# Weights' conversion from float64: a parametric Relu on ScalarE and one VectorE operation less

## The chip, the cores and the metric

One core of a Trainium2 chip runs the whole program. It has a TensorE (PE in the rows; PEld is its weight load), a VectorE (DVE), a ScalarE (ACT), a GpSimd (POOL) and a SyncE (SP) that issues the transfers. The metric is the device time of one execution in microseconds (us), and lower is better.

## The reference, cut to what matters

```python
kv  = einsum('bhsd,bhse->bhde', k, v)          # linear attention, 8 x 8 heads, 576 rows, 64 columns
out = einsum('bhsd,bhde->bhse', q, kv)
x   = out / sqrt(mean(out*out) + 1e-6) * g_norm    # -> 4608 tokens x 512

h = x @ w_in                                    # 512 x 2048
g = (a0 + a1*h + a2*h^2 + a3*h^3) / (1 + |b0||h| + |b1|h^2 + 1e-6)
x = g @ w_out                                   # 2048 x 512

return (((x @ w1) * (x @ w2)) @ w3) @ w_out2    # 512 x 1024 twice, 1024 x 1024, 1024 x 512
```

The activations q, k, v are float32. The six weight matrices are float64, since their float32 draw is scaled by a float64 factor. [...]

## The kernel before, in words

**Conversion.** `raw_load` brings a weight block of 128 x 512 float64 (512 KB) into a tile of pairs of words: `hw` is the high word (sign, 11 exponent bits, 20 mantissa bits) and `lw` the low word. `to_f32` makes a float32 tile `ct` of it in four operations. ScalarE reads `hw` as if it were a float32 and scales it by 2^-112, which corrects the exponent's offset and writes `ct` (line 149). VectorE cuts three bits out of the low word (line 151), shifts `ct` left by three and puts these bits in (line 155, into `lw`), and then puts the sign, which the shift has pushed out, back from the unshifted `ct` (line 159, into `ct`). Two more operations follow for the weights of the first two layers: ScalarE rounds `ct` to the high part (line 84) and VectorE subtracts for the low part (line 85). `conv` puts this pair into a list, `pend`, and `conv_on` runs it two conversions later, at the end of another block's `to_f32`.

**Where conversions stand.** There are 88. (1) 32 blocks of `w_in` (wa0 to wa15) and `w_out` (wb0 to wb15): 11 in an opening that is written out as a string of letters, one by one among the first attention tiles, and 21 in the first steps of the main loop (CONV gives how many in each step). (2) 32 half blocks of 128 x 256 of `w1` and `w2` (`bg_conv`) in the steps 64 and later. (3) 24 blocks of `w3` and `w_out2` (`cv_conv`, tile wb12) in the stage after the main loop.

**The main loop** has 192 steps g. Step g does on TensorE the 12 matmuls of layer one for one block of 128 hidden units and 384 tokens (`l1`, lines 88 to 90, into one of two PSUM tiles `h`), then the 12 of layer two of step g-3 (`l2`, lines 500 to 503), and between them matmuls of the attention of later tokens (lines 286, 347, 360, 403). The rational function is spread over ScalarE (lines 546 to 548, 562, 563, 536), GpSimd (line 550) and VectorE (lines 553, 555, 569, 571, 573, 538). Line 562 of a step waits for GpSimd's product of the same step, and `l1` of step g+2 waits for line 555 of step g, the last reader of that `h`.

**What sets the order.** Every engine works in program order. In a step, `mix` draws from generators in the order of a string; each letter runs one of them to its next `yield`, and what is left over runs at the end:

```python
MIX = "nntltsuysltsttunuuu", "snsnalttaltyasnt", "ntsnnltlsyttst"
```

The first string is for the steps with conversions of (1): n is lines 546 to 555, t, u and v are conversions, l the split of lines 536 and 538, y lines 562 and 563, s lines 569 to 573. The second is for those of (2). The opening runs each conversion as a whole.

Of the kernel before, what the change touches and what calls it, by code (L numbers as in the profile page):

```python
# [12 lines left out]
AF = mybir.ActivationFunctionType  # L13
ALU = mybir.AluOpType
# [4 lines left out]
def linear_attention_two_moe_kernel(  # L19
# [24 lines left out]
    nc = tc.nc  # L44
# [35 lines left out]
    def f32(ap):  # L80
        return ap.bitcast(F32)
# [62 lines left out]
    def to_f32(raw, t, n=W):  # L144


        hw, lw = raw[:, :, 1], raw[:, :, 0]
        ti = t.bitcast(I32)
        nc.scalar.activation(out=t, in_=f32(hw), func=AF.Copy, scale=2.0**-112)
        yield  # L150
        nc.vector.tensor_scalar(
            out=lw, in0=lw.bitcast(U32), scalar1=2.0**-29, scalar2=7.0, op0=ALU.mult, op1=ALU.min
        )
        yield
        nc.vector.scalar_tensor_tensor(
            out=lw, in0=ti, scalar=3, in1=lw, op0=ALU.logical_shift_left, op1=ALU.bitwise_or
        )
        yield
        nc.vector.scalar_tensor_tensor(
            out=ti, in0=ti, scalar=-0x80000000, in1=lw, op0=ALU.bitwise_and, op1=ALU.bitwise_or  # L160
        )

    def f32_tile(n=W):
# [16 lines left out]
    def conv(raw, *stages):  # L180

        t = f32_tile(W)
        yield from to_f32(raw, t)
        pend.append((t, list(stages)))
        conv_on()
# [231 lines left out]
    with tc.manual_schedule():  # L417
# [183 lines left out]
        for i in range(T0, NTILE):  # L601
            j, t = divmod(i, TPB)
# [30 lines left out]
        def bg_conv(n):  # L633
            w = f32_tile(HW)
            yield from to_f32(bg_raw.pop(n), w, HW)
            nc.sync.dma_start(out=bg[n][2], in_=w)
# [223 lines left out]
        def cv_conv(n):  # L860
            w = f32_tile()
            run(to_f32(cv_raw.pop(n), w))
            nc.sync.dma_start(out=cv[n][1], in_=w)
# [525 lines left out]
```

## Time and profile before

| | before |
|---|---|
| time, median of 3 runs (lowest, highest) | 1559.38 us (1557.82, 1559.94) |
| the profiled execution: time, span | 1558.43 us, 1556.7 us |
| TensorE busy, share of the span | 1515.8 us, 97% |
| VectorE | 1243.2 us, 80% |
| ScalarE | 1056.5 us, 68% |
| GpSimd | 225.0 us, 14% |

The span runs from the first instruction to the last. A busy TensorE is not a TensorE at its full rate, since a matmul's end in the trace is modelled, and the shares are means over stages with different limits. So what a VectorE operation is worth has to be read from the stage in which it stands.

### The profile page before, as it was taken

The numbers are of one execution on the slowest core, as the hardware profiler recorded it, in microseconds if no ns is written. First come the engines' busy times: TensorE is split into PE (matmuls) and PEld (weight loads), VectorE is DVE, ScalarE is ACT, GpSimd is POOL, SyncE is SP. The second block draws the span as 40 slices with busy tenths as digits, with TensorE's granted clock in tenths as the row PEclk, the third lists the DMA queues.
The fourth block names the chain that finished last, engine by engine and source line by source line (L and its number), as shares of the span: only waits on it lengthen the run. The fifth ranks groups of instructions, "written<-read, shape, count | busy, mean of one in ns | idle before, by whom it ended". The sixth has DMA issues, their size and how long they took to land.

```text
span 1556.7 us, 26099 instructions
## 1 busy us (share of the span) xinstructions
PE 1515.8 (97%) x9640; PEld 1477.4 (95%) x9640; DVE 1243.2 (80%) x2374; ACT 1056.5 (68%) x2109; POOL 225.0 (14%) x201
## 2 busy tenths in 40 slices
PE   4899999999999999999999999999999999999999
PEld 3788999999999999999999999999999999899999
DVE  5899968777889888988888889877677675688875
ACT  4688877787888888888888888544344343555554
POOL 0122221222222222222222221000000000000000
PEclk9799999999999999999999999999999999999999
DMA  9644243231112111110101021443543534434452
GB/s 281 194 141 140 72 112 99 82 96 45 48 38 69 42 45 42 45 55 28 58 28 56 6 69 37 146 146 112 190 141 117 190 119 164 140 110 154 155 160 89
DMA packets 153456, 157.95 MB, mean 101 GB/s; under 512 B 57328, under 2 KB 131312, under 8 KB 153328
## 3 DMA queue, kind: packets, MB, share of 16 engines
q1 hardware_dynamic: 153328, 156.28, 32.0%
q8 instruction: 76, 1.25, 0.3%
q14 instruction: 52, 0.43, 0.1%
HBM read 106.43 MB, written 49.81 MB: 100 GB/s over the span
## 4 chain that ended last, share of the span: by engine, by line
PE 85%; DVE 9%; ACT 3%; DMA 1%; issue 1%; POOL 1%; SPq 0%; DVEq 0%; POOLq 0%
PE acc L787 11%; PE h L88 8%; PE h L90 8%; PE h L89 8%; PE acc L500 7%; PE acc L501 7%; PE acc L503 7%; PE acc L1045 5%; PE h L787 5%; PE at L787 3%; PE kv L787 3%; PE h L1045 2%; PE kv L1045 2%; PE at L1045 2%; PE at L360 1%
## 5 line engine op out<-in xcount | busy, mean ns | idle before, releaser
L550 POOL TENSOR_TENSOR s<-z,a 128x384 f32<-128x384 f32 x192 | 223.3, 1163 | 732.6 <-ACT z L547 663.4
L553 DVE TENSOR_TENSOR n<-n,h 128x384 f32<-128x384 f32 x192 | 105.5, 550 | 91.9 <-ACT n L548 89.9
L546 ACT ACTIVATE a<-h 128x384 f32<-128x384 f32 x192 | 94.2, 491 | 98.3 <-PE h L90 97.6
L571 DVE SCALAR_TENSOR_TENSOR n<-n,na,y 128x384 f32<-128x384 f32 x192 | 155.4, 809 | 0.0
L562 ACT ACTIVATE y<-s,epsq 128x384 f32<-128x384 f32 x192 | 118.2, 616 | 44.7 <-POOL s L550 43.6
L547 ACT ACTIVATE z<-a,ab 128x384 f32<-128x384 f32 x192 | 136.2, 709 | 6.4
L548 ACT ACTIVATE n<-h,na 128x384 f32<-128x384 f32 x192 | 125.8, 655 | 0.0
L555 DVE SCALAR_TENSOR_TENSOR n<-n,na,h 128x384 f32<-128x384 f32 x192 | 116.4, 606 | 0.5
L569 DVE SCALAR_TENSOR_TENSOR s<-s,y 128x384 f32<-128x384 f32 x192 | 109.3, 569 | 0.0
L538 DVE TENSOR_TENSOR lo<-n,hi 128x384 fp32r<-128x384 f32 x192 | 106.9, 557 | 0.0
L573 DVE SCALAR_TENSOR_TENSOR n<-s,n 128x384 f32<-128x384 f32 x192 | 105.5, 550 | 0.2
L563 ACT ACTIVATE y<-y 128x384 f32<-128x384 f32 x192 | 101.0, 526 | 6.1
L536 ACT CAST hi<-n 128x384 fp32r<-128x384 f32 x192 | 96.1, 500 | 1.1 <-DVE n L573 1.1
L286 PEld LDWEIGHTS kv<-vt,kt 128*64 128x64 f32 (+1 forms) x640 | 24.7, 151 | 25.7 <-DMA kt<-in_k_dram 17.0
L286 PE MATMUL kv<-vt,kt 128*64 128x64 f32 (+1 forms) x640 | 30.4, 243 | 16.2 <-DMA vt<-in_v_dram 16.2
L829 ACT COPY p<-kv 128x384 f32<-128x384 f32 x24 | 11.5, 480 | 38.5 <-PE kv L787 26.9
L829 ACT COPY p<-acc 128x384 f32<-128x384 f32 x24 | 11.5, 480 | 38.5 <-PE acc L787 30.9
L844 ACT COPY u<-acc 128x384 f32<-128x384 f32 x24 | 11.5, 480 | 31.6 <-PE acc L787 31.6
L360 PE MATMUL at<-kvbd,qT 128*128 128x128 f32 (+1 forms) x216 | 29.2, 285 | 3.1 <-DVE kvbd L303 2.7
L360 PEld LDWEIGHTS at<-kvbd,qT 128*128 128x128 f32 (+1 forms) x216 | 26.6, 184 | 5.2 <-POOL s L550 3.0
L844 ACT COPY u<-h 128x384 f32<-128x384 f32 x24 | 11.5, 480 | 28.1 <-PE h L787 26.9
L379 DVE TENSOR_REDUCE ms<-sq 128x8 f32<-128x512 f32 x36 | 24.4, 683 | 5.9 <-ACT sq L373 5.9
(1440 smaller groups left out, 4923.0 us busy)
## 6 DMA issues: line engine op xcount, KB each, us to landing
ed<-eo SPq DMA_DIRECT2D x48, 384.0 KB, 2.6
er<-ed SPq DMA_DIRECT2D x35, 512.0 KB, 3.8
x2d<-xev SPq DMA_DIRECT2D x48, 192.0 KB, 2.0
xr<-x2d SPq DMA_DIRECT2D x48, 192.0 KB, 3.9
out_dram<-o SPq DMA_DIRECT2D x36, 256.0 KB, 2.0
kt<-in_k_dram SPq DMA_DIRECT2D x32, 256.0 KB, 2.8
vt<-in_v_dram SPq DMA_DIRECT2D x32, 256.0 KB, 3.2
qt<-in_q_dram SPq DMA_DIRECT2D x32, 256.0 KB, 3.1
```

The lines of the kernel that those rows point to most:

```text
L88: nc.tensor.matmul(outp, lhsT=lh, rhs=rh, start=first, stop=False)
L89: nc.tensor.matmul(outp, lhsT=lh, rhs=rl, start=False, stop=False)
L90: nc.tensor.matmul(outp, lhsT=ll, rhs=rh, start=False, stop=last)
L547: nc.scalar.activation(out=z, in_=a, func=AF.Identity, scale=ab[:, 1:2], bias=ab[:, 0:1])
L548: nc.scalar.activation(out=n, in_=h, func=AF.Identity, scale=na[:, 3:4], bias=na[:, 2:3])
L550: nc.gpsimd.tensor_tensor(out=s, in0=z, in1=a, op=ALU.mult)
L555: nc.vector.scalar_tensor_tensor(out=n, in0=n, scalar=na[:, 1:2], in1=h, op0=ALU.add, op1=ALU.mult)
L562: nc.scalar.activation(out=y, in_=e["s"], func=AF.Abs_reciprocal_sqrt, bias=epsq[:, 0:1])
L569: nc.vector.scalar_tensor_tensor(out=s, in0=s, scalar=EPS_Q, in1=y, op0=ALU.add, op1=ALU.mult)
L571: nc.vector.scalar_tensor_tensor(out=n, in0=n, scalar=na[:, 0:1], in1=y, op0=ALU.add, op1=ALU.mult)
L787: nc.tensor.matmul(bank, lhsT=lh[:, sl], rhs=x, start=first and kk == 0 and n == 0, stop=kk == 1 and n == 2, skip_group_check=True,)
L1045: nc.tensor.matmul(bank, lhsT=l[:, c, :], rhs=r, start=first and c == 0 and x == 0, stop=c == KH - 1 and x == 2, skip_group_check=True,)
```

## The change

ScalarE's scaling becomes a parametric Relu: inputs above zero are scaled by 2^-112 as before, and inputs below zero by 2^-112 times 2^32. The extra 2^32 adds 32 to a negative number's exponent field, which is bit 28 of the word, and the shift by three moves that bit to the sign's place, bit 31. So one VectorE operation both shifts and joins the low word's bits, and it writes `ct` directly; the second one goes, and with it one `yield`.

```diff
-        nc.scalar.activation(out=t, in_=f32(hw), func=AF.Copy, scale=2.0**-112)
+        nc.scalar.activation(out=t, in_=f32(hw), func=AF.Prelu, scale=2.0**-112, alpha=2.0**32)
         yield
         nc.vector.tensor_scalar(
             out=lw, in0=lw.bitcast(U32), scalar1=2.0**-29, scalar2=7.0, op0=ALU.mult, op1=ALU.min
         )
         yield
         nc.vector.scalar_tensor_tensor(
-            out=lw, in0=ti, scalar=3, in1=lw, op0=ALU.logical_shift_left, op1=ALU.bitwise_or
-        )
-        yield
-        nc.vector.scalar_tensor_tensor(
-            out=ti, in0=ti, scalar=-0x80000000, in1=lw, op0=ALU.bitwise_and, op1=ALU.bitwise_or
+            out=ti, in0=ti, scalar=3, in1=lw, op0=ALU.logical_shift_left, op1=ALU.bitwise_or
         )
```

The instruction lists of TensorE, ScalarE, GpSimd and SyncE are the same in both kernels, row for row (ScalarE's has one table load, at its head, in both). VectorE's has 88 rows less, 2310 against 2222, and in the steps with conversions some rows stand in another order. Lines behind the edit have numbers that are four lower in the changed kernel.

In the opening, this is VectorE's list before from the conversion of block wb1 to the first row sums of the attention tiles (line 379; wa4, wa5, wb0, wb1, wb2 are weight blocks, `r` marks the raw words, `hl` the two parts):

```order
L151 TENSOR_SCALAR wb1r<-wb1r 128x512
L155 SCALAR_TENSOR_TENSOR wb1r<-ct,wb1r 128x512
L159 SCALAR_TENSOR_TENSOR ct<-ct,wb1r 128x512
L85 TENSOR_TENSOR wb0hl<-ct,wb0hl 128x512
L151 TENSOR_SCALAR wa5r<-wa5r 128x512
L155 SCALAR_TENSOR_TENSOR wa5r<-ct,wa5r 128x512
L159 SCALAR_TENSOR_TENSOR ct<-ct,wa5r 128x512
L85 TENSOR_TENSOR wa4hl<-ct,wa4hl 128x512
L151 TENSOR_SCALAR wb2r<-wb2r 128x512
L155 SCALAR_TENSOR_TENSOR wb2r<-ct,wb2r 128x512
L159 SCALAR_TENSOR_TENSOR ct<-ct,wb2r 128x512
L85 TENSOR_TENSOR wb1hl<-ct,wb1hl 128x512
```

In the changed kernel the three rows of line 159 are gone here, and nothing else moves; the row sums of line 379 come next in both.

In the main loop, this is VectorE's list of one step with one conversion, before (step 20; s, n, lo, h are tiles of the rational function, wb14 and wb12 weight blocks):

```order
L151 TENSOR_SCALAR wb14r<-wb14r 128x512
L569 SCALAR_TENSOR_TENSOR s<-s,y 128x384
L571 SCALAR_TENSOR_TENSOR n<-n,na,y 128x384
L538 TENSOR_TENSOR lo<-n,hi 128x384
L155 SCALAR_TENSOR_TENSOR wb14r<-ct,wb14r 128x512
L573 SCALAR_TENSOR_TENSOR n<-s,n 128x384
L159 SCALAR_TENSOR_TENSOR ct<-ct,wb14r 128x512
L85 TENSOR_TENSOR wb12hl<-ct,wb12hl 128x512
L555 SCALAR_TENSOR_TENSOR n<-n,na,h 128x384
```

And the same step in the changed kernel:

```order
L151 TENSOR_SCALAR wb14r<-wb14r 128x512
L565 SCALAR_TENSOR_TENSOR s<-s,y 128x384
L567 SCALAR_TENSOR_TENSOR n<-n,na,y 128x384
L534 TENSOR_TENSOR lo<-n,hi 128x384
L155 SCALAR_TENSOR_TENSOR ct<-ct,wb14r 128x512
L85 TENSOR_TENSOR wb12hl<-ct,wb12hl 128x512
L569 SCALAR_TENSOR_TENSOR n<-s,n 128x384
L551 SCALAR_TENSOR_TENSOR n<-n,na,h 128x384
```

One row is gone, and the subtraction of line 85 now stands ahead of the last operation of the previous step's function (line 573 before, 569 after) instead of behind it.

## Rows read from the trace of the kernel before

**Rows 1.** Busy time by stage: start:end, length, then engines, clock, DMA share, GB/s.

```profile
core 0: us, PE busy (x) PEld busy (x) DVE busy (x) ACT busy (x) POOL busy (x), PEclk, DMA share, GB/s
16.00:48.00 32.00, 17.27 (x127) 14.71 (x128) 29.20 (x56) 19.59 (x39) 0.00 (x0) 0.87 0.89 270
...
87.40:169.30 81.90, 77.03 (x519) 71.03 (x517) 81.05 (x160) 72.65 (x137) 24.20 (x16) 1.00 0.44 135
...
250.00:820.00 570.00, 570.00 (x3530) 560.81 (x3529) 483.97 (x947) 468.07 (x914) 136.85 (x123) 1.00 0.18 53
...
980.00:1290.00 310.00, 310.00 (x1770) 309.88 (x1769) 219.04 (x417) 132.67 (x280) 0.00 (x0) 1.00 0.43 145
```

**Rows 2.** The chain that ended last, 103 to 170 us: shares by line.

```profile
by line: DMA wb14r<-in_moe_w_out_dram 6.5%; DVE n L571 6.3%; DVE n L555 6.3%; DVE ct L159 6.3%; DVE n L573 5.6%; DVE s L569 5.6%; issue 5.1%; POOL s L550 5.0%; DVE lo L538 3.8%; ACT z L547 3.2%; PE h L88 2.9%; ACT y L562 2.6%; ACT y L563 2.
```

**Rows 3.** TensorE's waits up to 160 us: us in total, times, longest.

```profile
PE h L88 <- DVE n L555: 5.8, 7, 2.1
PE acc L403 <- DVE xt L396: 5.3, 2, 3.7
```

**Rows 4.** Lines 149 and 159: nanoseconds least/median/most, first and last start.

```profile
L149 ACT ACTIVATE ct<-wb12r x25: 657/674/695, 150.4 to 1289.0; 128x512 f32<-128x512 f32 x25
...
L159 DVE SCALAR_TENSOR_TENSOR ct<-ct,str x32: 406/418/423, 256.0 to 818.4; 128x256 int32<-128x256 int32 x32
L159 DVE SCALAR_TENSOR_TENSOR ct<-ct,wb12r x25: 684/693/695, 154.6 to 1290.4; 128x512 int32<-128x512 int32 x25
```

**Rows 5.** ScalarE's first and second operation on `h`, groups of the page.

```profile
L546 ACT ACTIVATE a<-h 128x384 f32<-128x384 f32 x192 | 94.2, 491 | 98.3 <-PE h L90 97.6
...
L547 ACT ACTIVATE z<-a,ab 128x384 f32<-128x384 f32 x192 | 136.2, 709 | 6.4
```

**Rows 6.** The opening in order of time: start, duration, [idle before, what ended it].

```profile
29.10 1.12 PE L347 MATMUL acc<-ident,qt 128*128 128x128 f32 x4 [1.64 <-DMA qt<-in_q_dram]
...
30.48 0.68 ACT L149 ACTIVATE ct<-wb2r 128x512 f32<-128x512 f32 x1
...
32.15 0.60 ACT L373 ACTIVATE sq<-h 128x512 f32<-128x512 f32 x1
...
35.29 0.69 DVE L159 SCALAR_TENSOR_TENSOR ct<-ct,wb2r 128x512 int32<-128x512 int32 x1
35.90 0.68 DVE L85 TENSOR_TENSOR wb1hl<-ct,wb1hl 128x512 fp32r<-128x512 f32 x1
36.50 1.27 DVE L379 TENSOR_REDUCE ms<-sq 128x8 f32<-128x512 f32 x2
```

**Rows 7.** Step 1 in order of time: the long line 159 and TensorE's wait.

```profile
57.52 1.38 DVE L159 SCALAR_TENSOR_TENSOR ct<-ct,wb4r 128x512 int32<-128x512 int32 x1
...
64.70 1.94 PE L360 MATMUL at<-kvbd,qT 128*64 128x128 f32 x8 [2.75 <-DVE kvbd L303]
```

**Rows 8.** VectorE, line 555 of two successive steps; nine operations stand between.

```profile
155.80 0.61 DVE L555 SCALAR_TENSOR_TENSOR n<-n,na,h 128x384 f32<-128x384 f32 x1
...
160.86 0.61 DVE L555 SCALAR_TENSOR_TENSOR n<-n,na,h 128x384 f32<-128x384 f32 x1
```

**Rows 9.** Line 546, once a step, from step 6 to step 22.

```profile
L546 ACT ACTIVATE a<-h x17: 474/492/528, 87.4 to 169.3; 128x384 f32<-128x384 f32 x17
```

**Rows 10.** ScalarE in step 19 and the first operation of step 20.

```profile
153.81 0.49 ACT L546 ACTIVATE a<-h 128x384 f32<-128x384 f32 x1 [0.41 <-PE h L90]
...
156.79 0.62 ACT L562 ACTIVATE y<-s,epsq 128x384 f32<-128x384 f32 x1 [0.21 <-POOL s L550]
...
157.87 0.60 ACT L84 CAST wa15hl<-ct 128x512 fp32r<-128x512 f32 x1
158.88 0.50 ACT L546 ACTIVATE a<-h 128x384 f32<-128x384 f32 x1 [0.41 <-PE h L90]
```

**Rows 11.** TensorE's matmuls of line 286, and line 546 of two later steps.

```profile
155.79 0.69 PE L286 MATMUL kv<-vt,kt 128*64 128x64 f32 x16
...
416.90 0.49 ACT L546 ACTIVATE a<-h 128x384 f32<-128x384 f32 x1 [0.23 <-PE h L90]
...
421.10 0.49 ACT L546 ACTIVATE a<-h 128x384 f32<-128x384 f32 x1 [0.61 <-PE h L90]
```

**Rows 12.** Busy time and clock in two short stretches (columns as rows 1).

```profile
39.70:43.10 3.40, 1.83 (x8) 1.43 (x8) 2.97 (x8) 2.16 (x6) 0.00 (x0) 0.50 0.59 196
...
63.60:67.00 3.40, 2.29 (x9) 1.99 (x10) 3.34 (x8) 1.46 (x3) 0.83 (x1) 0.50 0.34 102
```

**Rows 13.** ScalarE's only table load.

```profile
L464 ACT ACT_TABLE_LOAD x1 | 1.3, 1283 | 0.7 <-PEq L1373 0.7
```

## Prediction

> **What bounds the kernel now.** I read the busy time by stage first, since VectorE's 80% is a mean. From 250 to 820 us TensorE is busy without a gap, and so it is from 980 to 1290 [rows 1]. All 32 half-block conversions lie in the first of these, from 256.0 to 818.4, and of the 25 with the tile wb12 one is a block of the second layer, at 154.6, and the 24 others belong to the stage behind the loop, up to 1290.4 [rows 4]. So their second VectorE operation runs beside a TensorE that waits for nothing. In the two earlier stretches it is the other way round: VectorE is busy 29.2 of 32 us from 16 to 48, while TensorE is busy 17.3, and 81.05 of 81.9 us from 87.4 to 169.3 [rows 1]. The reader is to see there an engine without a hole. The chain of work that ended last says the same of 103 to 170 us: line 159, which the change removes, lies on it with 6.3%, among five other VectorE lines [rows 2]. And TensorE's own waits up to 160 us name VectorE: 5.8 us for line 555, which releases an `h`, and 5.3 us for the normalized tile that is transposed first [rows 3]. So 32 of the 88 removed operations stand where VectorE sets the pace.
>
> **The change part by part.**
>
> *What is removed.* One operation of 128x512 costs 0.69 us by its own duration and one of 128x256 0.42 us [rows 4]. 24 of the first kind and all 32 of the second, 24 x 0.69 + 32 x 0.42 = 30 us, stand in the two stretches where TensorE has no gap: worth nothing. Were that cover gone, a step of the background conversions could win 0.42 us at most. The other 32 are counted by place.
>
> *Opening (11 conversions).* Eight of them, wa1 to wa3, wb0, wa4, wb1, wa5 and wb2, are done before the first row sums, which start at 36.50 [rows 6]. Eight times 0.69 would be 5.5 us, but not all can be had. The second row sum needs the square that ScalarE starts at 32.15; that square stands behind the attention matmuls of tile 1, and these behind a transposition that waited until 29.10 for q from DRAM [rows 6]. VectorE's work does not move that. ScalarE's scaling of wb2 starts at 30.48 and takes 0.68, so it ends at 31.16; one shift-and-join (0.69) and one subtraction of line 85 (0.60 from start to start, 35.90 to 36.50) follow, and the pair of row sums can start at 32.5 at the earliest, 4.0 us before now [rows 6]. I take 3.8, because ScalarE has a copy of a tile to do (as long as the square, 0.6) before it can use the first sum. The bounds are 3.0 (a quarter lost to transfers that are as late as now) and 4.0. The other three conversions of the opening end in VectorE's wait for the first step and count nothing; without that wait they would be worth 3 x 0.69.
>
> *Step 0 and 1.* Here the operation of line 159 took 1.38 us, twice its normal time [rows 7]. TensorE then waits 2.75 us for the copy of line 303, which stands behind this operation and the next block's [rows 7]. In the changed list both are gone: 1.38 + 0.69 = 2.1 us less as durations. One of the two lies next to an operation that could be stretched in its place, as line 159 was, so I take 1.6, bounds 0.6 and 2.1; the wait of 2.75 us holds it.
>
> *Steps 6 to 21 (16 steps, 16 conversions).* Line 546 runs once a step; 17 of them lie from 87.4 to 169.3, so a step takes 81.9 / 16 = 5.12 us [rows 9]. VectorE needs 160.86 - 155.80 = 5.06 us for its ten operations [rows 8], so nearly every step is VectorE's. With nine, the removed one counted from start to start as line 85 is (0.60), it needs 4.46. What is next? TensorE: a later step with 24 matmuls and nothing else takes 421.10 - 416.90 = 4.20, and every second step has line 286's matmuls besides, 0.69, so 4.20 + 0.35 = 4.55 [rows 11]. ScalarE: from its first operation at 153.81 to the end of line 84 at 157.87 + 0.60 is 4.66, with a wait of 0.21 for GpSimd inside; the 0.41 idle behind it is a wait for TensorE [rows 10]. So ScalarE's own 4.66 is the new floor of such a step, just above the other two, and the gain is 16 x (5.12 - 4.66) = 7.4 us. The bounds: 9.1 if only TensorE's 4.55 holds (16 x 0.57 = 9.1), and 4.2 with ScalarE at 4.86 (next paragraph). The moved subtraction (line 85 ahead of line 573) delays line 573 by one operation of 0.60 and saves one of 0.60 ahead of it: nothing. Its input, line 84, ends 4.66 us behind the step's start and VectorE gets to it some five us behind it (line 555 of step 19 starts at 160.86, 7.05 behind, three rows later in the new list), so no wait is added. Should ScalarE be late there, lines 573 and 555 queue behind it, and TensorE's `l1` two steps on behind line 555.
>
> *The scaling's new function.* No row has a parametric Relu. The scaling takes 0.674 us [rows 4]. On this engine two operations of one size differ most where one has per-row operands, 491 against 709 ns [rows 5]; the new one has constants alone, so I take 0, with bounds 0 and +0.2 us a conversion. At +0.2 a step of ScalarE takes 4.86. A gain has no ground: the old form is the simplest that there is.
>
> *The clock.* In 39.7 to 43.1 and in 63.6 to 67.0 the granted clock was 0.50, the lower level of 1.2 GHz; TensorE had been idle for 3.7 us before the first [rows 3] and 2.75 us before the second [rows 7, 12]. Both waits are among those that get shorter: the first by most of its length, the second to below 1 us. Twelve matmuls cost 2.1 us at the full clock (half of 4.20) and as much again at half [rows 11]. If both low stretches went, step 0's twelve would give 2.1 and step 3's twelve with the attention matmuls before them (1.94 at half [rows 7]) 2.1 + 1.0 = 3.1, so 5.2 in all; 0 if the clock falls as before. I take 1.5, half of the second.
>
> *Sum.* 3.8 + 1.6 + 7.4 + 1.5 = 14.3 us. Against the profiled execution, 1558.43, that is 1544.1; the median of the runs is 0.95 higher, so 1545.1.
>
> **The rivals.**
>
> *ScalarE and GpSimd hold the steps.* If the new function costs 0.2 more, the steps give 16 x (5.12 - 4.86) = 4.2, and with the opening at 3.8, step 1 at 0.6 and no clock, the gain is 8.6: 1550.8. For it: ScalarE is busy 72.65 of 81.9 us there [rows 1]. Against it: nothing but the function's table changes.
>
> *The clock stays up.* 3.8 + 2.1 + 7.4 + 5.2 = 18.5: 1540.9. For it: shorter waits. Against it: TensorE still waits in both places.
>
> *No change.* If the opening were paced by the transfers (DMA share 0.89 [rows 1]) and the steps by ScalarE at 5.0 or more, less than 3 us would be left: 1557 to 1559. Against it: VectorE has no idle time in the steps, and ScalarE waits in each [rows 10].
>
> *Table loads, slower.* If the parametric Relu is not in the table set in which the reciprocal square root is, each conversion needs a load before and one after it, at 1.28 us each [rows 13]. ScalarE's step would be 4.66 + 2.57 = 7.23 and the 16 steps 2.1 us longer each, 34 us; in a step of the background conversions ScalarE's 4.20 - 0.61 idle = 3.59 [rows 11] becomes 6.16, 32 x 1.96 = 63 us; so 1559.4 + 97 = 1656, and more with the opening. It decides from about seven such steps on (14.3 / 2.1). Against it: the changed ScalarE list has one load, at its head, as before. The Trainium skill (ScalarE activation tables: per-element evaluation and per-set limits, What a function is on this engine) has it that two functions of different sets are one load of 1283 ns apart, that those of one set need no switch, and that the same operands cost the same whichever table is read. The first figure is that of this trace's one load [rows 13]; by the last the +0.2 above would be nothing, and the sum would stay; no row here shows a parametric Relu.
>
> **How the numbers follow.** The forecast, gain 10 to 17, has 0.64; ScalarE's rival 0.14; the clock's 0.14; no change 0.05; table loads 0.03. The range takes in the first three: low, 1559.4 - 20.4 (4.0 + 2.1 + 9.1 + 5.2) = 1539; high 1559.4 - 7.8 (3.0 + 0.6 + 4.2 + 0) = 1551.6, so 1552. That leaves out the last two cases and the edges of others, in all under 2 in 10. Faster by over 0.2% (3.1 us, about what a measurement of this kernel can tell from no change) are the first three, 0.92; within it 0.05; slower 0.03.
>
> **What would show it.** The row sums of line 379 (375 in the changed kernel) start at 32.5 to 33 instead of 36.50. Line 546 (now 542) of step 6 comes 5 to 9 us earlier and the 16 steps behind it take 4.6 to 4.75 us each. VectorE shows holes in these steps, and waits of TensorE for the release of `h` nearly go. From step 64 on nothing changes but VectorE's busy time, 1243 - 88 operations (32 x 0.69 + 30) = 1191 us. Table loads beside the first, a scaling of over 0.8 us, or steps that stay at 5.0 would prove it wrong.

## The result, and the profile after

| | before | changed kernel |
|---|---|---|
| median, lowest to highest (4 runs each) | 1558.92 us, 1557.82 to 1559.94 | 1542.66 us, 1541.89 to 1546.83 |
| the profiled execution: time, span | 1558.43 us, 1556.7 us | 1546.83 us, 1545.0 us |

The ratio is 0.9901, with an interval from 0.9882 to 0.9920. The changed kernel was timed twice more beside other runs of the kernel before: 0.9912 (0.9899 to 0.9926) and 0.9913 (0.9900 to 0.9926). So the change takes 13 to 16 us off. The profiled execution is the slowest of its four, and its clock is read below.

The page of the changed kernel, busy times:

```profile
span 1545.0 us, 25977 instructions
PE 1510.7 (98%) x9640; PEld 1473.8 (95%) x9640; DVE 1193.5 (77%) x2286; ACT 1052.9 (68%) x2109; POOL 211.3 (14%) x201
```

VectorE has lost 49.7 us and GpSimd, of whose instructions not one was removed, 13.7 us. That second number is a first sign of something that the prediction had not counted.

Busy time by stage (columns as [rows 1]): the opening at the same times as there, then the same 16 steps and a stretch of the background stage.

```profile
16.00:48.00 32.00, 19.08 (x156) 15.92 (x157) 25.37 (x51) 20.45 (x42) 0.00 (x0) 0.89 0.98 285
82.30:157.70 75.40, 75.36 (x521) 71.12 (x519) 73.47 (x145) 71.53 (x136) 16.21 (x16) 1.00 0.48 147
240.00:806.00 566.00, 566.00 (x3508) 556.94 (x3507) 465.87 (x909) 464.48 (x909) 132.53 (x122) 1.00 0.18 53
```

In the opening VectorE is busy 25.37 of 32 us, where it was 29.20, and the DMA share has gone from 0.89 to 0.98. In the 16 steps TensorE is now the engine without a hole: 75.36 of 75.40 us. In the background stage TensorE is busy without a gap, as before.

TensorE's waits up to 160 us (us in total, times, longest), the first five:

```profile
PE kv L282 <- DMA vt<-in_v_dram: 18.2, 5, 9.4
PE acc L343 <- DMA qt<-in_q_dram: 2.7, 2, 2.1
PE at L356 <- ACT qT L348: 2.1, 3, 1.6
PE h L88 <- DVE n L551: 2.0, 1, 2.0
PE acc L399 <- DVE xt L392: 1.9, 2, 1.6
```

The release of `h` has fallen from seven waits with 5.8 us to one with 2.0, in step 1, and the normalized tile from 5.3 to 1.9 [rows 3]. Transfers of v led the list before, too, and they are no shorter now:

```profile
PE kv L286 <- DMA vt<-in_v_dram: 16.2, 5, 7.1
```

The chain of work that ended last, 16 to 48 us, shares by line, and its first pieces in order of time (start, us, what):

```profile
by line: DMA wa3r<-in_moe_w_in_dram 31.4%; DMA wb2r<-in_moe_w_out_dram 29.6%; DVE xt L392 8.7%; DVE ms L375 7.5%; DVE xl L408 4.1%; PE h L88 4.0%; issue 3.7%; PE at L399 3.4%; PE kv L282 3.3%; PE h L89 3.0%; PE h L90 2.7%; DVE ny L390 2.2%;
11.79 10.06 DMA wa3r<-in_moe_w_in_dram
21.87 9.48 DMA wb2r<-in_moe_w_out_dram
31.36 0.02 issue
31.38 0.69 ACT ct L149
32.07 0.02 issue
32.09 0.69 DVE ct L155
32.79 0.60 DVE wb1hl L85
33.39 1.20 DVE ms L375 x2
```

The row sums start when wb2, the last block ahead of them, has come, been scaled and joined, and line 85 has split an earlier one (wb1). There is no VectorE queue in front of them any more. The scaling of wb2 stood at 30.48 before, and its row lists no wait [rows 6]; here it waits for its block until 31.38:

```profile
31.38 0.68 ACT L149 ACTIVATE ct<-wb2r 128x512 f32<-128x512 f32 x1 [0.51 <-DMA wb2r<-in_moe_w_out_dram]
```

Where step g of the main loop begins (its first ScalarE operation, line 546 before) sorts the gain by place. Every kernel that was profiled stands in this table, the experiments too; the times are those of the profiled executions:

| profile | step 0 | step 3 | step 6 | step 22 | time | time less step 22 |
|---|---|---|---|---|---|---|
| before | 50.80 | 70.72 | 87.43 | 169.34 | 1558.43 | 1389.1 |
| prelu_two_ops | 50.81 | 70.49 | 87.20 | 169.11 | 1558.39 | 1389.3 |
| late_only | 48.49 | 68.66 | 85.38 | 167.29 | 1556.76 | 1389.5 |
| opening_only | 47.01 | 67.03 | 83.75 | 165.64 | 1555.37 | 1389.7 |
| steps_only | 49.90 | 68.73 | 85.43 | 160.91 | 1550.44 | 1389.5 |
| changed kernel | 46.81 | 65.64 | 82.36 | 157.78 | 1546.83 | 1389.1 |
| after_again | 45.33 | 62.47 | 79.03 | 154.50 | 1544.01 | 1389.5 |
| after_third | 44.76 | 62.45 | 78.98 | 154.46 | 1543.33 | 1388.9 |
| extra_yield | 47.64 | 64.34 | 80.25 | 155.61 | 1544.72 | 1389.1 |
| filler_reduce | 44.55 | 64.08 | 80.75 | 164.46 | 1553.09 | 1388.6 |
| warm | 45.70 | 63.13 | 79.56 | 155.01 | 1544.22 | 1389.2 |
| q_early | 46.97 | 65.62 | 81.54 | 157.00 | 1546.27 | 1389.3 |
| c_late | 45.83 | 65.45 | 82.00 | 157.40 | 1546.18 | 1388.8 |
| q_early_c_late | 45.72 | 63.34 | 79.26 | 154.69 | 1543.91 | 1389.2 |

The last column is flat within 1.1 us: what any of these kernels gains or loses lies ahead of step 22.

### The profile page after: what moved, and what is told of

It is laid out like the page before. It is cut to its first block, busy times and chain, and to the rows that moved or that the text cites. A ratio compares the mean times of both kernels' runs of the same rounds, so it can differ in the third digit from the quotient of the medians.

```text
span 1545.0 us, 25977 instructions
## 1 busy us (share of the span) xinstructions
PE 1510.7 (98%) x9640; PEld 1473.8 (95%) x9640; DVE 1193.5 (77%) x2286; ACT 1052.9 (68%) x2109; POOL 211.3 (14%) x201
## 4 chain that ended last, share of the span: by engine, by line
PE 90%; DVE 3%; ACT 2%; DMA 2%; issue 1%; POOL 1%; SPq 0%; DVEq 0%; POOLq 0%
PE acc L783 11%; PE h L88 9%; PE h L90 9%; PE h L89 9%; PE acc L496 8%; PE acc L497 8%; PE acc L499 8%; PE acc L1041 5%; PE h L783 5%; PE at L783 3%; PE kv L783 3%; PE h L1041 2%; PE kv L1041 2%; PE at L1041 2%; PE at L356 2%; PE kv L282 1%
## 5 line engine op out<-in xcount | busy, mean ns | idle before, releaser
L546 POOL TENSOR_TENSOR s<-z,a 128x384 f32<-128x384 f32 x192 | 209.6, 1092 | 734.3 <-ACT z L543 642.0
L831 DVE TENSOR_TENSOR eo<-c,kv 128x384 f32<-128x384 f32 x24 | 13.2, 552 | 22.5 <-PE kv L783 22.5
```

The source lines that it names most:

```text
L546: nc.gpsimd.tensor_tensor(out=s, in0=z, in1=a, op=ALU.mult)
```

## The experiments

No kernel here leaves out a part of the computation. Two do work besides that nobody uses: filler_reduce a row reduction, warm some matmuls.

**after_again, after_third: the changed kernel again.** No edit.

> The changed kernel once more, for its spread and its clock. Theory (the opening and the steps give what the profile shows, 11.6 us, and the rest is TensorE's clock): median near 1543, ratio near 0.990, and over the single runs the time falls as the granted clock of the span rises, about 0.8 us for each 0.001 that the clock rises (half of 0.002 of 1545 us is 1.5 us at the lower level, about half of it lost). Rival (the spread has nothing to do with the clock): no order between time and clock.

Measured: 1544.59 us (1544.01 to 1545.40, 4 runs), ratio 0.9912. The four runs show no order with their granted clock (1544.96 at 0.995, 1544.22 at 0.996, 1544.01 and 1545.40 at 0.997), where the expectation had a falling time. Over all 13 runs of the changed kernel there is a weak one: mean 1545.5 for the three at 0.995 and 1541.9 for the two at 0.999, but 1546.86 for one at 0.998. The 21 runs of the kernel before show it clearly: mean 1559.4 for the 8 runs at 0.993, 1558.1 for 6 at 0.995, 1556.5 for 6 at 0.996, and 1554.4 at 0.998.

> The changed kernel once more, on the chip of the three kernels beside it: 1542.5 to 1545.

Measured: 1544.61 us (1541.98 to 1546.86, 5 runs), ratio 0.9913. Three profiles of one program have step 0 at 46.81, 45.33 and 44.76, and need 18.83, 17.14 and 17.69 from step 0 to 3; the 16 steps behind step 6 are 75.42, 75.47 and 75.48. So the opening scatters by 2 us and the steps don't.

**prelu_two_ops: the new function with the old VectorE operations.** The slope is 1, so that the function changes nothing in the values.

```diff
-        nc.scalar.activation(out=t, in_=f32(hw), func=AF.Copy, scale=2.0**-112)
+        nc.scalar.activation(out=t, in_=f32(hw), func=AF.Prelu, scale=2.0**-112, alpha=1.0)
```

> ScalarE's parametric Relu with slope 1 (which scales all inputs alike) and both old VectorE operations. Theory (the new function costs what the old one did, no table loads, and the whole gain is VectorE's): the time of the kernel before, 1558 to 1560, one table load, scaling 0.66 to 0.69 us. Rival (a share of the gain comes from ScalarE's new function, or it costs something that the gain hides): 2 us or more off the kernel before.

Measured: 1558.36 us (11 runs), ratio 0.9996 (0.9987 to 1.0004). In a group of the lines view (us busy, mean ns | idle before, with what ended it), the scaling is:

```profile
L149 ACT ACTIVATE ct<-wb12r 128x512 f32<-128x512 f32 x25 | 16.9, 676 | 7.1 <-DMA wb12r<-in_moe_w_dram 6.3 <-DMA wb12r<-in_moe_w_out_dram 0.8
```

That is 676 ns in the mean, where the copy's median was 674 [rows 4]; in the changed kernel the mean is 673. The parametric Relu costs nothing here, and both kernels have one table load, as before. So the gain is not ScalarE's.

**late_only, opening_only, steps_only: the new form in one place alone.** A variable says where the program stands, and `to_f32` takes the new form in one stage and the old one in the others; of the three edits this is the one for the opening:

```diff
+        if stage[0] == "open":
+            nc.scalar.activation(out=t, in_=f32(hw), func=AF.Prelu, scale=2.0**-112, alpha=2.0**32)
...
+            return
+        nc.scalar.activation(out=t, in_=f32(hw), func=AF.Copy, scale=2.0**-112)
```

> The new form only in the 56 conversions from step 64 on and in the stage behind the loop. Theory (TensorE has no gap there): within 1.5 us of the kernel before, VectorE 30 us less busy. Rival (the late ones give a share of the gain, in proportion to VectorE's 30 of 50 us): 1550.

Measured: 1557.56 us (11 runs), ratio 0.9999 (0.9990 to 1.0008). VectorE is busy 1211.6 us, 31.6 less than before, and it buys nothing: the 56 late conversions run beside a TensorE that waits for nothing.

> The new form only in the 11 conversions of the opening. Theory: 3.5 to 5 us less than the kernel before (with luck in the clock up to 7), 1553 to 1556, the steps still 5.07 us each. Rival (the opening is paced by the transfers, and its conversions give nothing): 1558 to 1559.

Measured: 1553.32 us (5 runs), ratio 0.9963 (0.9949 to 0.9977). The row sums start at 32.62, step 0 at 47.01, and the 16 steps keep their 81.89.

> The new form only in the 21 conversions of the steps 0 to 21. Theory (steps 6 to 21 go from 5.12 to 4.71 us because TensorE's own work is the next bound, and step 1 gives 1 to 2): 7.5 to 9 us less than the kernel before, 1549.5 to 1551, and with the opening's share (about 5.5 us) the sum is the whole change's 14 to 15. Rival (the parts are not additive, since a step's speed depends on the opening's transfers): less than 6 us.

Measured: 1548.53 us (5 runs), ratio 0.9938 (0.9925 to 0.9952). The 16 steps take 75.48, step 0 to 3 takes 18.83. The parts add up: 5.3 us below their kernel before for the opening and 9.85 for the steps make 15.1, and the whole had 12.7 to 16.3. The steps gave a little more than was expected of them (1549.5 to 1551).

**extra_yield: the order of before.** One `yield` more at the end of `to_f32` puts line 85 behind the previous step's last operation again (line 573 before).

```diff
             out=ti, in0=ti, scalar=3, in1=lw, op0=ALU.logical_shift_left, op1=ALU.bitwise_or
         )
+        yield
```

> The changed kernel with the yield put back behind the joining operation, so that line 85 stands behind the last operation of the previous step's function as before. Theory (the move is worth nothing, the removed operation is worth all): within 1.5 us of the changed kernel, 1543 to 1546. Rival (the move lets line 85, and so the release of h, come in better time): 1547 or more, steps of 4.8 us or more.

Measured: 1543.54 us (4 runs), ratio 0.9906 (0.9893 to 0.9920), 16 steps in 75.36. The move that came with the change is worth nothing that these runs can tell, as the prediction had it.

**filler_reduce: VectorE's time given back with another operation.** In the steps a row reduction of `ct`, which reads one tile, stands where line 159 stood. Its result isn't used.

```diff
+        if stage[0] == "steps":
+            yield
+            nc.vector.tensor_reduce(
+                out=junk, in_=t.rearrange("p (a b) -> p a b", a=8), axis=AX.X, op=ALU.add
+            )
```

> The changed kernel with a row reduction of one tile (one SBUF input, 0.68 us by line 379, result unused) in the steps' conversions where the removed operation stood. Theory A (VectorE's time per step is what counts): steps back to 5.05 us, 1550 to 1552, and GpSimd's product 1.0 us if it is two-input operations that stretch it, 1.6 if it is only their number. Theory B (a good part of the gain was GpSimd's shorter product, 1.0 against 1.6 us, which ScalarE waited for): steps of 4.7 to 4.85, 1545 to 1547, with a product of 1.0.

Measured: 1553.19 us (8 runs), ratio 0.9971 (0.9961 to 0.9981). Steps 13 to 20 take 5.05 to 5.08 again, with as many VectorE operations that read two tiles as in the changed kernel. Busy time from 87 to 168 us, which covers them (columns as [rows 1]):

```profile
87.00:168.00 81.00, 74.03 (x504) 68.26 (x504) 80.97 (x156) 69.62 (x131) 22.22 (x16) 1.00 0.43 127
```

VectorE is without a hole again, and ScalarE is not. So it is VectorE's time that the steps had been paying for. Rows of one step, in order of time (start, us, engine, [idle before, what ended it]):

```profile
144.68 0.68 DVE L162 TENSOR_REDUCE junk<-ct 128x8 f32<-128x512 f32 x1
...
145.21 1.62 POOL L555 TENSOR_TENSOR s<-z,a 128x384 f32<-128x384 f32 x1 [3.44 <-ACT z L552]
145.28 0.68 DVE L85 TENSOR_TENSOR wa14hl<-ct,wa14hl 128x512 fp32r<-128x512 f32 x1
...
145.88 0.61 DVE L560 SCALAR_TENSOR_TENSOR n<-n,na,h 128x384 f32<-128x384 f32 x1
...
146.86 0.62 ACT L567 ACTIVATE y<-s,epsq 128x384 f32<-128x384 f32 x1 [0.21 <-POOL s L555]
```

GpSimd's product takes 1.62 us here, with line 85 beside it, and ScalarE waits 0.21 for it, just as before the change [rows 10]. The expectation had taken 1.6 as a sign that the number of VectorE's operations stretches the product; it had not counted that line 85, which reads two tiles, would fall beside it. Since the slow product came back together with the operation, this run alone does not part the two; the busy times above do.

**warm: the clock held up in the opening.** TensorE fills four of its waits with 21 matmuls of the identity, into tiles that are written over afterwards. The edit for 13 of them, in three waits of the opening (the other 8 stand ahead of step 3's matmuls):

```diff
+        if i < T0:
+            for p in range(WARM[i]):
+                nc.tensor.matmul(px[:, p % KD, :], lhsT=ident, rhs=ident, start=True, stop=True)
```

> The changed kernel with 21 matmuls of the identity in TensorE's waits of the opening and of step 3, into PSUM tiles that are overwritten right after. Theory (the spread between runs and some us of the early steps are TensorE's lower clock): no stretch at the lower clock between 36 and 66 us, 1 to 4 us less than the changed kernel, 1541 to 1543. Rival (the early steps are paced by transfers and VectorE, and a lower clock hides in the waits): within 1 us of the changed kernel, or slower by the 3 us that the matmuls take.

Measured: 1543.85 us (4 runs), ratio 0.9908 (0.9894 to 0.9921), which is inside what the changed kernel gives and not the 1541 to 1543 of the theory. Up to 66 us one stretch at 0.50 is left (the level of 1.2 GHz), by the windows view:

```profile
48.50:51.90 3.40, 3.40 (x16) 3.30 (x12) 2.33 (x5) 2.22 (x5) 0.00 (x0) 0.50 0.96 314
```

It stands behind another wait, for v:

```profile
47.98 0.34 PE L282 MATMUL kv<-vt,kt 128*64 128x64 f32 x4 [2.31 <-DMA vt<-in_v_dram]
```

Step 0 is at 45.70, between the changed kernel's, and takes 6.82 us, where it takes 4.92 in the changed kernel's profile, which has no such wait there. As these rows read, what the clock gave back was waited for at the next transfer.

**q_early, c_late, q_early_c_late: a shorter way to the row sums.** The opening's order is a string; Q loads a q tile, W loads a weight block, C converts one. The first puts the third Q ahead of three weight blocks, the second moves the conversion of wb2 (the opening's ninth, with wa0) behind the row sums, and the third does both:

```diff
-... "KQKWKcKdkQkCtWCWkCWCFkKWkWCCWCWQWtCQoCtoKWtKWKrrooWWKQknrrKnnxxkWnxWCQkCxW"
+... "KQKWKcKdkQkCtWCWkCWCFkKWkQWCCWCWWtCQotoKWtKWKrrooWWKQknrrKnnxxkWnxWCCQkCxW"
```

> The changed kernel with the load of the third q tile moved ahead of three weight blocks in the opening. Theory (with VectorE's operations gone the opening waits for transfers, for wb2 above all, which lands no earlier here): row sums of line 375 at 31.5 to 33, TensorE's wait for q gone, 0 to 1.5 us less than the changed kernel. Rival (the square behind that q tile is what the row sums wait for, as the prediction said): 2 to 3 us less.

Measured: 1543.37 us (5 runs), ratio 0.9907 (0.9894 to 0.9921). The row sums start at 34.21, later and not earlier.

> The changed kernel with the conversion of wb2 moved behind the row sums and normalizations of the opening's tiles. Theory (both the conversion of wb2 and the square hold the row sums, within 1 us of each other): row sums at most 1 us earlier, 0 to 1 us less than the changed kernel. Rival (wb2 alone holds them): 2 us less.

Measured: 1544.89 us (4 runs), ratio 0.9915 (0.9902 to 0.9929). The first row sum starts at 32.19, but the second at 34.02, behind a wait of 1.16 for its square.

> Both moves. Theory (two things hold the row sums at nearly the same time, so both have to go): row sums at 30 to 31, and 1.5 to 3 us less than the changed kernel, 1541 to 1543, unless the k and v transfers that come later in the queue hold step 1 instead, as they did for 2.3 us in one of the runs. Rival (the next transfers take all of it): within 0.5 us of the changed kernel.

Measured: 1544.59 us (4 runs), ratio 0.9916 (0.9902 to 0.9929). The row sums start at 31.06, 2.2 us ahead of the changed kernel's profile, and step 0 at 45.72, 1.1 ahead; but after_again and after_third have step 0 at 45.33 and 44.76. The next wait is this one:

```profile
48.25 0.36 PE L282 MATMUL kv<-vt,kt 128*64 128x64 f32 x5 [2.56 <-DMA vt<-in_v_dram]
```

So none of the three beats the changed kernel, and the 1541 to 1543 expected of the last did not come. As the rows read, what is won ahead of one transfer is waited for at the next: after_again, too, waits 2.37 us for v at 47.66, and the changed kernel's profile, with step 0 at 46.81, has no such wait there.

## Why the prediction was right, and where its steps were off

The forecast was 1545.1 us, and the three medians are 1542.66, 1544.59 and 1544.61. Its sign, its places and its size hold; the engine that it named as the steps' next limit does not. I take each term from the table, as the mean over four profiles with the old form in that place less the mean over four with the new one (the three of the changed kernel and the one that changes this place alone).

| stretch | predicted | old form | new form | measured |
|---|---|---|---|---|
| up to step 0 | 3.8 | 50.00 | 45.98 | 4.0 |
| steps 0 to 2 | 1.6 and the clock's 1.5 | 19.95 | 18.12 | 1.8 |
| steps 3 to 5 | 0 | 16.72 | 16.63 | 0.1 |
| steps 6 to 21 | 7.4 | 81.91 | 75.46 | 6.4 |
| the 56 late conversions | 0 | | | 0 |
| the new function, the moved row | 0 | | | 0 |

The clock's term belongs to steps 0 to 2, since the matmuls of step 3, which it counts, stand ahead of line 546 of that step (in the kernel before they run from 66.57 to 70.68, and line 546 starts at 70.72). The terms sum to 12.3, against 14.3 by the mean of the three differences of medians (16.3, 14.0, 12.7); the opening's scatter of 2 us is as large as the rest. That the medians give the forecast's 14.3 to the tenth is therefore luck.

*The opening: right in size, and its floor is a transfer.* The row sums start at 33.30, 32.05, 32.91 and 32.62, where 32.5 to 33 was forecast. In the four kernels the scaling of wb2 starts at 31.38, 30.08, 30.97 and 30.70, each within 0.03 us of the landing of its block, and the row sums follow it by 1.92 to 1.97, as the prediction's 0.68 + 0.69 + 0.60 has it. So the transfer is the floor. It is not later for the change: with the old form in the opening the same scaling starts at 30.48, 31.29, 31.57 and 30.34, just as close behind the landing, and only the row sums come later (36.10 to 36.97). The prediction held this start fixed at 30.48, and it scatters by over 1 us. (The conversions ahead of the row sums are nine, with wa0, and not eight; since the transfer sets the floor, the sum does not depend on it.)

*Steps 0 and 1: the price of a stretched operation stays.* The prediction took less than the full 2.1 us because a neighbour could be stretched in place of line 159 [rows 7]. That is what happened, in the changed kernel's step 1:

```profile
52.81 0.69 DVE L155 SCALAR_TENSOR_TENSOR ct<-ct,wb4r 128x512 int32<-128x512 int32 x1
...
53.03 1.35 POOL L546 TENSOR_TENSOR s<-z,a 128x384 f32<-128x384 f32 x1 [3.88 <-ACT z L543]
...
53.41 1.51 DVE L85 TENSOR_TENSOR wb3hl<-ct,wb3hl 128x512 fp32r<-128x512 f32 x1
```

Line 85 takes 1.51 us, where it takes 0.68 alone [rows 6]. From the start of step 0 to the copy of line 303 (299 now) it is 12.14 us instead of 13.33, so 1.2 of the forecast 1.6. In after_again line 85 was not stretched (0.68).

*The steps: the step that failed is "ScalarE's own 4.66 is the new floor of such a step".* The size was near (4.71 a step, 4.66 forecast), but the engine was another. In the changed kernel ScalarE's row of eight operations comes round in 4.25 us without a wait between them:

```profile
138.94 0.49 ACT L542 ACTIVATE a<-h 128x384 f32<-128x384 f32 x1 [0.50 <-PE h L90]
...
140.06 0.60 DVE L551 SCALAR_TENSOR_TENSOR n<-n,na,h 128x384 f32<-128x384 f32 x1
...
140.28 1.01 POOL L546 TENSOR_TENSOR s<-z,a 128x384 f32<-128x384 f32 x1 [3.57 <-ACT z L543]
...
140.77 0.55 DVE L549 TENSOR_TENSOR n<-n,h 128x384 f32<-128x384 f32 x1
...
141.59 0.62 ACT L558 ACTIVATE y<-s,epsq 128x384 f32<-128x384 f32 x1
...
142.68 0.60 ACT L84 CAST wb11hl<-ct 128x512 fp32r<-128x512 f32 x1
...
143.19 0.49 ACT L542 ACTIVATE a<-h 128x384 f32<-128x384 f32 x1
```

The 4.66 had been read from a step in which GpSimd's product was slow, and so it held a wait of 0.21 for that product; it also counted line 84 to its end (0.60) where the next operation starts 0.51 behind it. The product is the key. One of it before, and then as a group over the 16 steps, before and in the changed kernel:

```profile
155.12 1.64 POOL L550 TENSOR_TENSOR s<-z,a 128x384 f32<-128x384 f32 x1 [3.44 <-ACT z L547]
...
155.19 0.69 DVE L85 TENSOR_TENSOR wb11hl<-ct,wb11hl 128x512 fp32r<-128x512 f32 x1
```

```profile
L550 POOL TENSOR_TENSOR s<-z,a 128x384 f32<-128x384 f32 x16 | 24.2, 1512 | 58.9 <-ACT z L547 49.5 <-DVE xt L396 4.9 <-DVE n L573 4.4
```

```profile
L546 POOL TENSOR_TENSOR s<-z,a 128x384 f32<-128x384 f32 x16 | 16.2, 1013 | 60.7 <-ACT z L543 31.3 <-DVE n L569 29.4
```

In the mean it takes 1.01 us instead of 1.51, since line 85 no longer falls beside it. Before, 14 of the 16 products have line 85 beside them and take 1.18 to 1.80, and the two others take 1.01; in the changed kernel none has it, and all take 1.00 to 1.03. In filler_reduce line 85 falls beside it again, and it takes 1.62. The moved row is not the reason: with the old order put back (extra_yield) the mean is 1.07. The Trainium skill (SBUF — State Buffer, Who interferes with whom) has it that a VectorE instruction with two inputs in SBUF contends with a GpSimd instruction that reads SBUF, and one with at most one such input, outside the two-port modes, does not. The trace agrees: line 85 reads two tiles from SBUF and costs the product 0.6 us, while lines 551 and 549, which read one and the PSUM tile `h`, fall beside it at 140.06 and 140.77 and cost it nothing.

The floor is TensorE's. It waits for nothing from 82.3 to 157.7, and steps 13 to 20 alternate between 4.25 to 4.27 and 4.95 to 5.02, which is the prediction's 4.20 and 4.20 + 0.69 [rows 11] and a little. Their mean is 4.62 where it had 4.55. The other eight are less even (4.31 to 5.37), with transpositions for the attention in some of them, and make the mean 4.71. That is the missing 1.0 us of the 7.4. VectorE is close behind: 73.47 of 75.40 us. So the holes that the prediction gave as a sign hardly came, 1.9 us in 16 steps against 0.9 before. The forecast 4.46 for its nine operations is borne out by filler_reduce, where one more of 0.60 from start to start makes 5.06.

*The clock: a term of the right size, in two of four profiles.* In the profiled changed kernel the granted clock is 0.50 for 13.7 us of the first 66, and in the profile of before for 20.5 of the first 71. The low stretch that matters lies in steps 0 to 2. Where it lasts 6.8 us, as in all four profiles with the old form, these steps take 18.83 (the changed kernel and steps_only), 1.1 less than 19.95. In after_again and after_third it lasts 3.4 (57.4 to 60.8 and 57.6 to 61.0), and they take 17.14 and 17.69, so 1.1 to 1.7 less again. The forecast 1.5 was of the right size where the stretch was halved and nothing where it was not; this is read from the profiles and was not forced. The waits did shorten as forecast, from 3.7 to 1.6 and from 2.75 to 1.5 (the second low stretch of before began at 63.6, inside the wait that ended at 64.70 and not behind it [rows 7, 12]), but in the changed kernel's profile the clock fell there all the same, at 38.5 and at 59.0. Warm, which took most of the low stretches away, gained no more than the changed kernel has without it.

*The rivals.* ScalarE and GpSimd did not hold the steps, and prelu_two_ops excludes the dearer function and the table loads. "No change" fell with the 6.4 us of the steps. "The clock stays up" would need a clock without low stretches, and each of the changed kernel's three profiles has two up to 66 us. What stays open is the changed kernel's own spread, 1541.9 to 1546.9: it arises ahead of step 22 in the three profiles, it follows the mean clock of the span only weakly, and no experiment held it still.

## What to carry to other kernels

Count the removed operations by the stage in which they stand: 32 of 88 made the whole gain here, and 56 bought 31.6 us of idle VectorE. When the full engine is relieved, work the next floor out from the durations that its neighbours have when undisturbed: a wait or a stretched operation inside the row that is measured belongs to the old state. In this opening, which loads at a DMA share of 0.98, a shorter way on one engine ended at the next transfer, and three reorderings gained nothing.

## What was not expected of the hardware

Who pays when line 85 meets GpSimd's product differs from step to step, and their starts alone do not settle it. With line 85 starting 0.07 us behind the product, the product takes 1.62 and line 85 its usual 0.68. With line 85 starting 0.38 behind, in the changed kernel's step 1, line 85 takes 1.51 and the product 1.35; the product's 0.34 above its usual 1.01 lies beside line 155, which reads two tiles, too, and started 0.22 ahead of it. But in step 2 of the kernel before, with the same 0.38 (62.52 and 62.90), the product takes 1.92 and line 85 0.68. The case with 1.51 is like the Trainium skill's rule (SBUF — State Buffer, SBUF: two separate sides) that the one that starts first keeps the shared ports and the other waits. The case of 0.07 is not, as far as GpSimd's recorded starts can be trusted to 0.07 us; in filler_reduce line 85 pays (1.32 to 1.48, with a product of 1.02) in three steps where it starts 0.08 or 0.24 behind. Why the product paid at 0.38 stays open.

A parametric Relu with a slope of 2^32 costs on ScalarE what a copy with a scale costs (mean 673 ns in the changed kernel, median 674 before, for 128x512), so a factor that depends on the sign cost nothing here.
